# A gated-convolution and ELU kernel: products of TensorE on 64 rows, two halves side by side

## The chip, the cores and the metric

The kernel runs on one core of one Trainium2 chip. The metric is device microseconds of the whole program; the kernel before takes 1214.82 us, the median of 3 runs.

## What is computed

A softmax-weighted causal convolution over 7 tokens (8 heads of 24 features) and a two-layer network with ELU between the layers, all in float32:

```python
w = softmax(weight_gen, axis=-1)                      # (4, 4096, 8, 7)
x_pad = np.concatenate([zeros(B, 6, D), x], axis=1)   # x: (4, 4096, 192)
conv[b, s, h, :] = sum over k of w[b, s, h, k] * x_pad[b, s + k, h, :]
x = conv.reshape(16384, 192)
h = x @ w_in                                          # w_in (192, 2048)
g = np.where(h > 0, h, np.exp(np.minimum(h, 0)) - 1)
out = g @ w_out                                       # w_out (2048, 192)
```

## The kernel before

The 16384 tokens are cut into 32 blocks of 512 tokens (N = 512), and the 2048 hidden features into 16 f-tiles of 128. So there are 512 steps, each one f-tile of one block. A float32 product is made of fp32r products of high and low parts: each operand is split into hi, its value rounded to fp32r, and lo = value - hi, and hi·hi + hi·lo + lo·hi are summed in PSUM.

`f_tile` holds one step. `mm1` (L560) makes h = w_in·x with five products of 128 rows and 512 columns: of the 192 features 128 (32 from each of four quadrants) lie in `xhi` and `xlo`, three products; the other 64 lie twice in `xd`, once as hi and once as lo, which needs two. Then the ELU: ScalarE makes relu(-h) (L567) and exp (L569), VectorE combines them (L571), ScalarE rounds to `hi` (L574), VectorE subtracts to `lo` (L576). `mm2` (L589) multiplies with w_out, five products again: three into the PSUM bank `acc` (128 output features) and two into `accd` (the other 64, whose hi and lo weights lie side by side, so that the two halves of `accd` are added in the drain). `mm2` of a step follows `mm1` of a step four f-tiles later (`LA = 4`), so that the ELU runs beside other products. `h` has three PSUM banks, `acc` and `accd` two each.

Before a block's products, `chunk` loads x and the convolution's weights (four loads each, for two blocks at a time after the first two) and makes the softmax; `conv` sums the seven taps on GpSimd (blocks 0 and 1 in `summed`, with TensorE adding up in PSUM); `split` transposes the sum on VectorE (two instructions of 512 columns) and makes `xhi`, `xlo`, `xd`. After a block's last product `drain` adds the halves of `accd`, transposes both sums on VectorE and stores them. `weights` decodes the weights from 64-bit words during block 0; the 64 extra rows of w_in are doubled by products with `picks` (L353). `turn_over` keeps TensorE busy with products of the identity at the start.

All of this goes through `Plan`: each operation is a task with an engine, a cost and a due time; `issue` lays the tasks out by due time on a model of the engines and then emits them in the order of their modelled starts. That order is each engine's instruction order, and SP's queue of loads and stores as well. `due1(s)` is the due time of step s.

The order of the steps is blocks 0 and 1 in turns of 8, 4 and 4 f-tiles, then block by block.

Of the kernel before, what the change touches and what calls it, by code (L numbers as in the profile page):

```python
# [22 lines left out]
class Ring:  # L23
# [6 lines left out]
    def new(self):  # L30
        h = Handle(self.make)
# [100 lines left out]
def conv_elu_kernel(  # L132
# [16 lines left out]
    Q = 4  # L149
    A = P // Q  # L150
# [4 lines left out]
    E = DQ - A  # L155
# [3 lines left out]
    J = N // A  # L159
    JH = J // 2  # L160
    NB = T * R // J
    D1 = D - P
    FILL = 24
# [3 lines left out]
    LA = 4  # L167

    sizes = [J, J] + [2 * J] * (T * R // (2 * J) - 1)
    starts = [sum(sizes[:i]) for i in range(len(sizes))]  # L170
    CM = max(sizes)
    chunk_of = {st // J + i: (c, i * J) for c, (st, n) in enumerate(zip(starts, sizes))
                for i in range(n // J)}

    def rows(ap, t0, n):

        return ap.rearrange("(a r) t d -> r a t d", r=R)[t0 // T][:, t0 % T:t0 % T + n]

# [7 lines left out]
    count = const.tile([P, 1], I32, name="count")  # L186
    second = const.tile([P, 1], F32, name="second")


    row = const.tile([P, 1], F32, name="row")  # L190
    rows_i = const.tile([P, 1], I32, name="rows_i")
    ids = const.tile([P, P], I32, name="ids")
    col = const.tile([P, P], F32, name="col")
    picks = [const.tile([P, P], F32, name=f"pick{i}") for i in range(2)]

    WC = 2 * P + D
    W = const.tile([P, NF, 2 * WC], F32R, name="W")
    D_HI, A_HI, O_HI, O_BOTH, A_LO, O_LO, D_LO = (slice(c, c + P) for c in range(0, 7 * P, P))  # L200
    in_pieces = {0: 2, 2: 2, **{f: 4 for f in range(4, NF, 4)}}
# [4 lines left out]
    r_raw_in = ring("raw_in", [P, 6 * P, 2], 3, I32)  # L206
    r_m_in = ring("m_in", [P, 6 * P], 2, I32)
    r_raw_out = ring("raw_out", [P, 2 * D, 2], 4, I32)
    r_m_out = ring("m_out", [P, 2 * D], 3, I32)
    r_xw = ring("xw", [P, HALO + CM, DQ], 2)  # L210
    r_wg = ring("wg", [P, CM, H, K], 2)
    r_wm = ring("wm", [P, CM, H, 1], 1)
    r_ws = ring("ws", [P, CM, H, 1], 1)
    r_pa = ring("pa", [P, J, H, G], 2)
    r_pb = ring("pb", [P, J, H, G], 1)
    r_v = ring("v", [P, JH, H, G], 6)
    r_xc = ring("xc", [P, J, H, G], 2)
    r_xt = ring("xt", [P, 2, J * A], 1)
    r_xhi = ring("xhi", [P, N], 2, F32R)
    r_xlo = ring("xlo", [P, N], 2, F32R)  # L220
    r_xd = ring("xd", [P, N], 2, F32R)
    r_xr = ring("xr", [P, N], 1, F32R)
    r_e = ring("e", [P, N], 3)
    r_hi = ring("hi", [P, N], 4, F32R)
    r_lo = ring("lo", [P, N], 4, F32R)
    r_cr = ring("cr", [D1, N], 1)
    r_ot = ring("ot", [P, J, A], 2)
    r_od = ring("od", [D1, J, A], 2)
    r_h = ring("h", [P, N], 3, pool=ps)
    r_wd = ring("wd", [P, 4, P], 1, pool=ps)  # L230
    r_acc = ring("acc", [P, N], 2, pool=ps)
    r_accd = ring("accd", [P, N], 2, pool=ps)
# [4 lines left out]
    idle = r_acc.new()  # L237
# [21 lines left out]
    STEP = 10 * pe(N)  # L259
    T0 = 20000  # L260

    def due1(s):
        return T0 + s * STEP


# [3 lines left out]
    def weights(f0, nf, of_in, own_q=None):  # L269


        raw, m = (r_raw_in.new(), r_m_in.new()) if of_in else (r_raw_out.new(), r_m_out.new())
        hi_h, lo_h = Handle(), Handle()
        fs = W[:, f0:f0 + nf]
        wide = P if of_in else D
        na = nf * wide
        nh = nf // 2
        n = na + (nh * P if of_in else 0)
        for f in range(f0, f0 + nf):
            (w_in_h if of_in else w_out_h)[f] = [hi_h, lo_h]  # L280

        def m_(c=slice(0, n)):
            return m.t[:, c]

        def mf(c=slice(0, n)):
            return m_(c).bitcast(F32)

        def own(c):
            return mf(slice(0, na)).rearrange("p (f m) -> p f m", f=nf)[:, :, c]
# [4 lines left out]
        def load_out():  # L294
            nc.sync.dma_start(
                out=raw.t[:, 0:na].rearrange("p (f m) w -> p f (m w)", f=nf),
                in_=moe_w_out.bitcast(I32)[f0 * P:(f0 + nf) * P, :].rearrange(
                    "(f p) m -> p f m", p=P))

        w = moe_w_in.bitcast(I32).rearrange("(q e) m -> q e m", q=Q)  # L300

        def load_in(eng):
            for q in range(Q):
                eng.dma_start(
                    out=raw.t[q * A:(q + 1) * A, 0:na].rearrange("p c w -> p (c w)"),
                    in_=w[q, 0:A, 2 * f0 * P:2 * (f0 + nf) * P])

        def load_rest():
            for i in range(2):
                at = f0 + i * nh  # L310
                nc.sync.dma_start(  # L311
                    out=raw.t[i * D1:(i + 1) * D1, na:n].rearrange("p c w -> p (c w)"),
                    in_=w[:, A:DQ, 2 * at * P:2 * (at + nh) * P])

        if not of_in:
            add("dma", max(dma(nf * P, 8 * D), ISSUE), load_out, writes=[raw])
        elif own_q:

            begun = Handle()
            add("pool", Q * 1000, lambda: load_in(own_q), writes=[raw, begun])  # L320
            add("dma2", 0, lambda: None, reads=[begun], writes=[raw])
            add("dma", max(dma(P, nh * 8 * P), 2 * ISSUE), load_rest, writes=[raw])
        else:
            add("dma", max(dma(P, 8 * na), Q * ISSUE), lambda: load_in(nc.sync), writes=[raw])
            add("dma", max(dma(P, nh * 8 * P), 2 * ISSUE), load_rest, writes=[raw])
# [17 lines left out]
        if of_in:  # L343
            wd, d_hi, d_lo = r_wd.new(), Handle(), Handle()
            for f in range(f0, f0 + nf):
                w_in_h[f] += d_hi, d_lo

            def wds():
                return wd.t[:, 0:nf]

            def pick():
                for i in range(2):
                    nc.tensor.matmul(out=wd.t[:, i * nh:(i + 1) * nh], lhsT=picks[i],  # L353
                                     rhs=mf(slice(na, n)), start=True, stop=True)

            add("pe", 2 * 4 * pe(nh * P), pick, reads=[m], writes=[wd], due=due1(f0) - 2000)
            add("act", act(nf * P, True), lambda: nc.scalar.copy(out=fs[:, :, D_HI], in_=wds()),
                reads=[wd], writes=[d_hi])
            add("dve", dve(nf * P), lambda: nc.vector.tensor_tensor(
                out=fs[:, :, D_LO], in0=wds(), in1=fs[:, :, D_HI].bitcast(F32), op=ALU.subtract),  # L360
                reads=[wd, d_hi], writes=[d_lo])
        to = A_HI if of_in else slice(O_HI.start, WC)
        add("act", act(na), lambda: nc.scalar.copy(out=fs[:, :, to], in_=own(slice(0, wide))),
            reads=[m], writes=[hi_h])
        parts = ((slice(0, P), A_HI, A_LO),) if of_in else (
# [336 lines left out]
```

## Time and profile before

| | us |
|---|---|
| median of 3 runs | 1214.82 (1213.92 to 1215.94) |
| span of the profiled execution, first to last instruction | 1212.2 |
| TensorE products busy | 1196.1 (99%) |
| TensorE weight loads busy (beside the products) | 984.2 (81%) |
| ScalarE busy | 927.8 (77%) |
| VectorE busy | 898.4 (74%) |
| GpSimd busy | 710.1 (59%) |

A record of a TensorE product is longer than its pace: products are pipelined, and each record begins before its predecessor's has ended. The pace is the distance between starts. A weight load is a record of its own (PEld). Between the profiled span and the median lie 2.6 us.

### The profile page before, as it was taken

How to read it: one execution, taken by the hardware profiler on the slowest of the kernel's cores; microseconds unless marked ns; L12 is line 12 of the kernel's file. 1: busy time of each engine (PE TensorE's matmuls, PEld its weight loads, DVE VectorE, ACT ScalarE, POOL GpSimd, SP SyncE). 2: the span in 40 equal slices, each digit the busy share in tenths (PEclk: the TensorE clock that was granted, in tenths of full speed). 3: DMA queues.
4: the chain of work that ended last, by engine and by line, in shares of the span. 5: the costliest groups of instructions: out<-in, count | busy, mean ns of one | idle time of the engine just before them, and what ended most of it. 6: DMA issues, size and time to landing. Idle time of an engine off the chain costs nothing.

```text
span 1212.2 us, 15948 instructions
## 1 busy us (share of the span) xinstructions
PE 1196.1 (99%) x5268; PEld 984.2 (81%) x5268; DVE 898.4 (74%) x1411; ACT 927.8 (77%) x1716; POOL 710.1 (59%) x442
## 2 busy tenths in 40 slices
PE   8999999999999999999999999999999999999997
PEld 7687888888888888888888888787888888888886
DVE  7977777777787776777677786777777677777765
ACT  5887878777777777777777787777777777787775
POOL 4678393863919458292764909459292774909500
PEclk9999999999999999999999999999999999999999
DMA  7820404004040320404003040220403104000001
GB/s 157 140 33 14 53 14 52 14 10 44 14 52 14 38 28 1 52 14 52 15 13 40 14 52 14 31 31 6 52 14 47 20 9 44 14 14 14 14 9 18
DMA packets 251514, 38.66 MB, mean 32 GB/s; under 512 B 248168, under 2 KB 250472, under 8 KB 251432
## 3 DMA queue, kind: packets, MB, share of 16 engines
q1 hardware_dynamic: 251304, 37.39, 23.1%
q8 instruction: 41, 0.67, 0.2%
q14 instruction: 41, 0.34, 0.1%
q0 software_dynamic: 128, 0.26, 0.1%
HBM read 25.05 MB, written 12.58 MB: 31 GB/s over the span
## 4 chain that ended last, share of the span: by engine, by line
PE 94%; DMA 3%; DVE 1%; SPq 1%; ACT 1%; issue 1%; ACTq 0%
PE h L560 47%; PE acc L589 28%; PE accd L589 19%; DMA raw_in<-in_moe_w_in 2%; SPq L403 1%; DMA xw<-in_x 1%; DVE xd L547 0%; ACT e L567 0%; SPq L311 0%; DVE xlo L547 0%; ACT hi L574 0%; ACT e L569 0%; DVE lo L576 0%; ACT xhi L542 0%; DVE h L571 0%
## 5 line engine op out<-in xcount | busy, mean ns | idle before, releaser
L576 DVE TENSOR_TENSOR lo<-h,hi 128x512 fp32r<-128x512 f32 x512 | 353.8, 691 | 239.1 <-ACT hi L574 195.5
L567 ACT ACTIVATE e<-h 128x512 f32<-128x512 f32 x512 | 307.5, 601 | 158.8 <-PE h L560 157.1
L560 PE MATMUL h<-xd,W 128*128 128x512 f32 x1024 | 401.0, 392 | 4.9 <-DVE xd L547 4.1
L589 PE MATMUL acc<-hi,W 128*128 128x512 f32 x1024 | 399.4, 390 | 0.0
L560 PE MATMUL h<-xhi,W 128*128 128x512 f32 x1024 | 398.5, 389 | 0.0
L571 DVE SCALAR_TENSOR_TENSOR h<-e,h 128x512 f32<-128x512 f32 x512 | 351.9, 688 | 59.2 <-ACT e L569 59.0
L574 ACT CAST hi<-h 128x512 fp32r<-128x512 f32 x512 | 298.8, 584 | 94.0 <-DVE h L571 92.9
L569 ACT ACTIVATE e<-e 128x512 f32<-128x512 f32 x512 | 328.2, 641 | 4.5
L434 POOL TENSOR_TENSOR pb<-xw,wg 128x768 f32<-128x768 f32 x182 | 287.3, 1578 | 11.5
L449 POOL TENSOR_TENSOR pa<-pa,pb 128x768 f32<-128x768 f32 x150 | 282.1, 1880 | 11.7
L434 POOL TENSOR_TENSOR pa<-xw,wg 128x768 f32<-128x768 f32 x32 | 49.5, 1548 | 371.6 <-DVE wg L424 366.2
L560 PEld LDWEIGHTS h<-xd,W 128*128 128x128 f32 x1024 | 192.2, 188 | 48.7 <-DVE xd L547 5.8
L589 PEld LDWEIGHTS acc<-hi,W 128*128 128x128 f32 x1024 | 192.3, 188 | 40.0
L560 PEld LDWEIGHTS h<-xhi,W 128*128 128x128 f32 x1024 | 192.3, 188 | 39.8
L589 PE MATMUL accd<-hi,W 128*128 128x512 f32 x512 | 199.5, 390 | 0.6 <-POOL W L370 0.6
L560 PE MATMUL h<-xlo,W 128*128 128x512 f32 x512 | 199.2, 389 | 0.0
L589 PE MATMUL accd<-lo,W 128*128 128x512 f32 x512 | 199.2, 389 | 0.0
L589 PE MATMUL acc<-lo,W 128*128 128x512 f32 x512 | 199.2, 389 | 0.0
L589 PEld LDWEIGHTS accd<-hi,W 128*128 128x128 f32 x512 | 96.1, 188 | 21.7 <-POOL W L370 1.8
L560 PEld LDWEIGHTS h<-xlo,W 128*128 128x128 f32 x512 | 96.1, 188 | 20.0
L589 PEld LDWEIGHTS accd<-lo,W 128*128 128x128 f32 x512 | 96.1, 188 | 20.0
L589 PEld LDWEIGHTS acc<-lo,W 128*128 128x128 f32 x512 | 96.1, 188 | 20.0
(81 smaller groups left out, 514.3 us busy)
## 6 DMA issues: line engine op xcount, KB each, us to landing
xw<-in_x SPq DMA_DIRECT2D x60, 228.0 KB, 4.9
out_dram<-ot SPq DMA_DIRECT2D x128, 64.0 KB, 2.0
out_dram<-od SPq DMA_DIRECT2D x64, 64.0 KB, 1.9
wg<-in_weight_gen SPq DMA_DIRECT2D x60, 56.0 KB, 3.0
raw_out<-in_moe_w_out SPq DMA_DIRECT2D x8, 384.0 KB, 7.1
raw_in<-in_moe_w_in SPq DMA_DIRECT2D x18, 128.0 KB, 5.1
xw<-in_x SPq DMA_DIRECT2D x8, 132.0 KB, 4.5
raw_in<-in_moe_w_in SPq DMA_DIRECT2D x8, 64.0 KB
```

Of the source, the lines that this page charges most:

```text
L403: nc.sync.dma_start(out=to()[q * A:(q + 1) * A], in_=rows(src, t0, n)[:, :, q * d:(q + 1) * d])
L434: lambda: eng.tensor_tensor(out=h.t, in0=xw.t[:, j0 + k:j0 + k + J, :].rearrange("p j (h g) -> p j h g", g=G), in1=wg.t[:, j0:j0 + J, :, k ...
L449: add("pool", pool(J * DQ), lambda b=b, to=to: nc.gpsimd.tensor_tensor(out=to.t, in0=a.t, in1=b.t, op=ALU.add), reads=[b] if to is a else ...
L560: nc.tensor.matmul(out=h.t, lhsT=W[:, f, w], rhs=r.t, start=(i == 0), stop=(i == len(pairs) - 1))
L567: add("act", act(N, True), lambda: nc.scalar.activation(out=e.t, in_=h.t, func=ACTF.Relu, scale=-1.0), reads=[h], writes=[e])
L569: add("act", act(N), lambda: nc.scalar.activation(out=e.t, in_=e.t, func=ACTF.Exp, scale=-1.0), writes=[e])
L571: add("dve", dve(N), lambda: nc.vector.scalar_tensor_tensor(out=h.t, in0=e.t, scalar=-1.0, in1=h.t, op0=ALU.add, op1=ALU.max), reads=[e], ...
L574: add("act", act(N, True), lambda: nc.scalar.copy(out=hi.t, in_=h.t), reads=[h], writes=[hi])
L576: add("dve", dve(N), lambda: nc.vector.tensor_tensor(out=lo.t, in0=h.t, in1=hi.t.bitcast(F32), op=ALU.subtract), reads=[h, hi], writes=[lo])
L589: nc.tensor.matmul(out=to.t, lhsT=W[:, f, w], rhs=r.t, start=(first and r is hi and w != O_LO), stop=(last and r is lo), skip_group_check= ...
```

## The change

There are no full-array products with w_in any more. A block's 512 tokens are laid out as two halves of 256: the lower 64 partitions hold the 192 features (as `C = 3` parts of 64 rows) of the first half, the upper 64 those of the second. Copies by DMA in `split` (`other`) bring each half's tokens to the other partitions too, so that each half of the rows has all 512 columns. The f-tiles go in pairs: one f-tile's w_in lies on the lower rows, the other's on the upper rows (`WI`), and each f-tile takes nine products of 64 rows (3 terms x 3 parts). The doubled rows, `picks` and `xd` go.

In blocks 0 and 1 the nine products of one f-tile alternate with those of the other, and w_out's ten products per pair stay full. From block 2 on (`APART`) w_out's product is cut in two by its 128 hidden rows: the upper 64 rows' half (`up`) runs two pairs later beside the w_in products of the pair's lower f-tile, the lower half (`down`) three pairs later beside those of the upper f-tile. Each half has its own banks `acc` and `accd`, one of each per half where there were two for all; `drain` runs once per half, with two transposes each, and the halves are added on GpSimd, as are the two halves of `accd`. `h` has four banks, `hi` and `lo` seven buffers. x and the convolution's weights are loaded block by block, in eight pieces each. The planner's step is a pair of f-tiles of 19 product costs. The diff, cut to its core:

```diff
-    Q = 4
-    A = P // Q
+    Q, S = 2, 2
+    A = P // (Q * S)
...
-    E = DQ - A
+    C = DQ // A
...
-    LA = 4
...
+    LAG = 2
+    APART = range(2, NB)
...
+    WI = const.tile([P, NP, 2, C, P], F32R, name="WI")
+    WO = const.tile([P, NF, 3 * P], F32R, name="WO")
...
+    r_xw = ring("xw", [P, HALO + J, DQ], 3)
+    r_wg = ring("wg", [P, J, H, K], 3)
...
+    r_xhi = ring("xhi", [P, C, 3, NS], 2, F32R)
+    r_xlo = ring("xlo", [P, C, 3, NS], 2, F32R)
...
-    r_hi = ring("hi", [P, N], 4, F32R)
-    r_lo = ring("lo", [P, N], 4, F32R)
...
-    r_h = ring("h", [P, N], 3, pool=ps)
...
-    r_acc = ring("acc", [P, N], 2, pool=ps)
-    r_accd = ring("accd", [P, N], 2, pool=ps)
+    r_hi = ring("hi", [P, N], 7, F32R)
+    r_lo = ring("lo", [P, N], 7, F32R)
+    r_cr = ring("cr", [D1, S * J, A], 1)
+    r_h = ring("h", [P, N], 4, pool=ps)
+    r_acc = [ring(f"acc{i}", [P, N], 1, pool=ps) for i in range(2)]
+    r_accd = [ring(f"accd{i}", [P, N], 1, pool=ps) for i in range(2)]
...
-    STEP = 10 * pe(N)
+    STEP = 19 * pe(N)
...
+                for p, s, q in quadrants():
+                    nc.sync.dma_start(out=to()[p],
+                                      in_=rows(src, t0 + s * J, n)[:, :, q * d:(q + 1) * d])
...
+            for c in range(C):
+                def turn(i=i, c=c, xc=xc):
...
+                    nc.vector.transpose(out=xt(i)[:, c], in_=src[:, :, c * A:(c + 1) * A])
+                add("dve", dve(n * A), turn, reads=[xc], writes=[xts[i], part], due=due)
+            done = Handle()
+            add("act", act(C * n * A), lambda i=i: nc.scalar.copy(out=to(xhi, i), in_=xt(i)),
+                reads=[xts[i], part], writes=[xhi, done])
+            add("dve", dve(C * n * A), lambda i=i: nc.vector.tensor_tensor(
+                out=to(xlo, i), in0=xt(i), in1=to(xhi, i).bitcast(F32), op=ALU.subtract),
+                reads=[xts[i], part, done], writes=[xlo], port=blk > 0)
+        low, high = slice(0, HALF), slice(HALF, P)
+        for x in (xhi, xlo):
+            def other(x=x):
+                t = x.t.bitcast(I32)
+                nc.sync.dma_start(out=t[high, :, 0], in_=t[low, :, 1])
+                nc.sync.dma_start(out=t[low, :, 2], in_=t[high, :, 1])
+            add("dma", max(dma(P * C, 4 * NS), 2 * ISSUE), other, writes=[x])
...
+    def product_in(blk, k, i, h):
+        xhi, xlo = xt_h[blk]
+        p, c0 = ((low, 1), (high, 0))[i]
+        terms = [(w, x, c) for w, x in ((1, xhi), (0, xlo), (0, xhi)) for c in range(C)]
+        def one(at):
+            w, x, c = terms[at]
+            return lambda: nc.tensor.matmul(
+                out=h.t, lhsT=WI[p, k, w, c], rhs=x.t[p, c, c0:c0 + 2].rearrange(
+                    "p s n -> p (s n)"), start=(at == 0), stop=(at == len(terms) - 1),
+                skip_group_check=True)
+        return [one(at) for at in range(len(terms))]
+    whole = slice(0, P)
+    def banks(blk, p):
+        return acc_h[blk][1 if p is high else 0]
+    def product_out(blk, k, p):
+        acc, accd = banks(blk, p)
+        out = []
+        for i, f in enumerate(pair_of[k]):
+            hi, lo = elu_h[blk, f]
+            for to, w, r in ((accd, O_BOTH, hi), (accd, O_BOTH, lo), (acc, O_HI, hi),
+                             (acc, O_LO, hi), (acc, O_HI, lo)):
+                def run(f=f, to=to, w=w, r=r, hi=hi, i=i):
+                    nc.tensor.matmul(
+                        out=to.t, lhsT=WO[p, f, w], rhs=r.t[p],
+                        start=(k == 0 and i == 0 and r is hi and w != O_LO),
+                        stop=(k == NP - 1 and i == 1 and r is not hi), skip_group_check=True)
+                out.append(run)
+        return out
...
+    def period(s, now, up, down):
...
+        n = 3 * C
+        if now:
+            blk, k = now
+            h = [r_h.new(), r_h.new()]
+            fs = pair_of[k]
+            reads = [*w_in_h[k], *xt_h[blk]]
+            t0, t1 = (product_in(blk, k, i, h[i]) for i in range(2))
+        if up:
+            blk2, k2 = up
+            if k2 == 0:
+                acc_h[blk2] = [(r_acc[i].new(), r_accd[i].new())
+                               for i in ((1, 0) if blk2 in APART else (blk2,))]
+        if up and up[0] not in APART:
+            if now:
+                add("pe", n * pe(N), run(*pairs(t0, t1)), reads=reads, writes=h, due=due1(s))
+            add("pe", 10 * pe(N), run(*product_out(*up, whole)), reads=ready(blk2, pair_of[k2]),
+                writes=[x for y in acc_h[blk2] for x in y], due=due1(s) + STEP / 2)
+            if now:
+                for f, x in zip(fs, h):
+                    elu(blk, f, x)
+            return
...
+        def side(mine, m2, p, hr, h, at):
+            out = product_out(*m2, p) if m2 else []
+            to = banks(m2[0], p) if m2 else []
+            of = pair_of[m2[1]] if m2 else ()
+            ahead = p is low
+            for a, b, f in ((0, 5, of[0:1]), (5, 10, of[1:2])):
+                todo = [x for i in range(a, b) for x in (
+                    out[i:i + 1] + mine[i:i + 1] if ahead else mine[i:i + 1] + out[i:i + 1])]
+                slots = b - a - (ahead and a == 0)
+                add("pe", slots * pe(N), run(*todo),
+                    reads=[*hr, *(ready(m2[0], f) if m2 else ())],
+                    writes=[*h, *to], due=due1(s) + (at + a) * pe(N))
+        if now:
+            side(t0, up, high, reads, h[0:1], 0)
+            elu(blk, fs[0], h[0])
+            side(t1, down, low, reads, h[1:2], 9)
+            elu(blk, fs[1], h[1])
...
+    def drain(blk, s1, p):
+        late = due1(s1 + 5)
+        soon = due1(s1 + 1)
+        sums = sums_h.setdefault(blk, [])
+        for acc, accd in [banks(blk, p)]:
+            each = []
+            for src in (accd, acc):
+                o = r_raw_out.new(by_token)
+                add("dve", dve(N), lambda o=o, src=src: nc.vector.transpose(
+                    out=o.t.rearrange("p j c -> p (j c)"), in_=src.t),
+                    reads=[src], writes=[o], due=soon)
+                each.append(o)
+            sums.append(each)
+        if p is high:
+            return
+        od, ot = sums[0]
+        for other in sums[1:]:
+            for to, o in zip((od, ot), other):
+                add("pool", pool(N), lambda to=to, o=o: nc.gpsimd.tensor_tensor(
+                    out=to.t, in0=to.t, in1=o.t, op=ALU.add), reads=[o], writes=[to], port=True,
+                    due=late)
+        cr = r_cr.new()
+        add("act", act(N), lambda: nc.scalar.copy(out=cr.t, in_=od.t[D1:P]),
+            reads=[od], writes=[cr], due=late)
+        add("pool", pool(N), lambda: nc.gpsimd.tensor_tensor(
+            out=od.t[0:D1], in0=od.t[0:D1], in1=cr.t, op=ALU.add), reads=[cr], writes=[od],
+            port=True, due=late)
+...
+    cuts = (0, 4, 6, NP)
+    runs = [(blk, k0, k1) for k0, k1 in zip(cuts, cuts[1:]) for blk in range(2)]
+    runs += [(blk, 0, NP) for blk in range(2, NB)]
+    todo = [(blk, k) for blk, k0, k1 in runs for k in range(k0, k1)]
...
+        for s in range(len(todo) + LAG + 1):
+            now = todo[s] if s < len(todo) else None
+            up = todo[s - LAG] if LAG <= s < len(todo) + LAG else None
+            down = todo[s - LAG - 1] if s > LAG else None
+            if down and down[0] not in APART:
+                down = None
...
+            period(s, now, up, down)
+            if up and up[1] == NP - 1:
+                drain(up[0], s, high if up[0] in APART else whole)
+            if down and down[1] == NP - 1:
+                drain(down[0], s, low)
```

## Rows read from the trace of the kernel before

**Rows 1.** The page: busy time by engine, and the ended-last chain by line.

```profile
PE 1196.1 (99%) x5268; PEld 984.2 (81%) x5268; DVE 898.4 (74%) x1411; ACT 927.8 (77%) x1716; POOL 710.1 (59%) x442
...
PE h L560 47%; PE acc L589 28%; PE accd L589 19%; DMA raw_in<-in_moe_w_in 2%; SPq L403 1%; DMA xw<-in_x 1%; DVE xd L547 0%; ACT e L567 0%; SPq L311 0%; DVE xlo L547 0%; ACT hi L574 0%; ACT e L569 0%; DVE lo L576 0%; ACT xhi L542 0%; DVE h L571 0%
```

**Rows 2.** Timeline, TensorE, near 600 us (start us, length us, engine line op).

```profile
600.05 0.39 PE L560 MATMUL h<-xhi,W 128*128 128x512 f32 x1
600.27 0.39 PE L560 MATMUL h<-xlo,W 128*128 128x512 f32 x1
...
602.31 0.39 PE L560 MATMUL h<-xhi,W 128*128 128x512 f32 x1
```

**Rows 3.** Groups by line and form, TensorE (count, busy us, mean ns, idle before).

```profile
L589 PE MATMUL acc<-hi,W 128*128 128x512 f32 x1024 | 399.4, 390 | 0.0
...
L353 PE MATMUL wd<-m_in,pick 128*128 128x256 f32 x12 | 3.1, 379 | 0.0
```

**Rows 4.** Busy time per stretch, engines in the order PE, PEld, DVE, ACT, POOL; clock.

```profile
400.00:600.00 200.00, 200.00 (x884) 165.68 (x883) 147.23 (x230) 155.34 (x289) 114.10 (x68) 1.00 0.24 30
```

**Rows 5.** All waits of TensorE (total us, times, longest).

```profile
PE h L560 <- DVE xd L547: 4.1, 4, 2.3
PE acc L485 <- DVE v L497: 2.6, 2, 1.7
PE acc L378 <- POOL ident masks.py:199: 1.4, 1, 1.4
PE h L560 <- DVE lo L576: 0.8, 1, 0.8
PE accd L589 <- POOL W L370: 0.6, 2, 0.4
```

**Rows 6.** Timeline, TensorE, the fillers and the first w_in product.

```profile
18.03 2.84 PE L378 MATMUL acc<-ident 128*128 128x128 f32 x24
20.63 0.49 PE L560 MATMUL h<-xd,W 128*128 128x512 f32 x1
```

**Rows 7.** Timeline, weight loads, of the same stretch.

```profile
17.92 2.76 PEld L378 LDWEIGHTS acc<-ident 128*128 128x128 f32 x24
20.62 0.19 PEld L560 LDWEIGHTS h<-xd,W 128*128 128x128 f32 x1
20.73 0.19 PEld L560 LDWEIGHTS h<-xhi,W 128*128 128x128 f32 x1
```

**Rows 8.** Timeline, weight loads, near 600 us.

```profile
600.05 0.19 PEld L560 LDWEIGHTS h<-xlo,W 128*128 128x128 f32 x1
```

**Rows 9.** Timeline, SP, the first issues.

```profile
0.75 1.97 SPq L403 DMA_DIRECT2D wg<-in_weight_gen  x4
2.76 2.54 SPq L403 DMA_DIRECT2D xw<-in_x  x4
```

**Rows 10.** Groups by line and form, VectorE and GpSimd.

```profile
L608 DVE STREAM_TRANSPOSE ot<-acc 128x512 f32<-128x512 f32 x32 | 22.7, 709 | 1.9 <-PE acc L589 1.9
...
L370 POOL TENSOR_TENSOR W<-m_in,W 128x512 fp32r<-128x512 f32 x3 | 3.9, 1296 | 0.0
...
L538 DVE STREAM_TRANSPOSE h<-acc 128x256 f32<-128x256 f32 x2 | 0.8, 444 | 0.3 <-PE acc L485 0.3
```

**Rows 11.** The page: DMA issues (count, KB each, us to landing).

```profile
out_dram<-od SPq DMA_DIRECT2D x64, 64.0 KB, 1.9
```

**Rows 12.** Timeline, last product and last store.

```profile
1205.23 0.39 PE L589 MATMUL acc<-lo,W 128*128 128x512 f32 x1
...
1208.44 1.00 SPq L615 DMA_DIRECT2D out_dram<-od  x2
```

**Rows 13.** Timeline, VectorE, a block's second subtract in `split`.

```profile
615.23 2.26 DVE L547 TENSOR_TENSOR xd<-xt,xr 128x512 fp32r<-128x512 f32 x1
```

**Rows 14.** Timeline, last product of an f-tile's h and the end of its ELU.

```profile
609.79 0.39 PE L560 MATMUL h<-xhi,W 128*128 128x512 f32 x1
...
613.55 0.68 DVE L576 TENSOR_TENSOR lo<-h,hi 128x512 fp32r<-128x512 f32 x1
```

More of the change, by code (lines that the diff above doesn't have):

```diff
@@ L184, in conv_elu_kernel @@
     scratch = const.tile([P, 1], F32, name="scratch")
[L186 to L199, printed above, removed]
@@ L257, in dma, with due1, decoded @@
         return packets * max(9 + byts / 12, 22) / 16
-    STEP = 10 * pe(N)
+    STEP = 19 * pe(N)
     T0 = 20000
-    def due1(s):
-        return T0 + s * STEP
+    def due1(k):
+        return T0 + k * STEP
     w_in_h, w_out_h = {}, {}
[L269 to L289, printed above, removed]
+    def decoded(raw, m, n):
@@ L291, in word @@
         def word(i):
             return raw.t[:, 0:n, i]
[L294 to L325, printed above, removed]
+        def m_():
+            return m.t[:, 0:n]
@@ L342, in weights @@
             out=m_(), in0=m_(), in1=word(0), op=ALU.add), reads=[raw, tail], writes=[m])
[L343 to L361, printed above, removed]
@@ new lines, in weights_out, with load, own @@
+    def weights_out(fs):
+        raw, m = r_raw_out.new(), r_m_out.new()
+        hi_h, lo_h = Handle(), Handle()
+        for f in fs:
+            w_out_h[f] = [hi_h, lo_h]
+        f0, step, nf = fs[0], fs[1] - fs[0], len(fs)
+        n = nf * D
+        to = WO[:, f0:fs[-1] + 1:step]
+        def load():
+            nc.sync.dma_start(
+                out=raw.t[:, 0:n].rearrange("p (f m) w -> p f (m w)", f=nf),
+                in_=moe_w_out.bitcast(I32).rearrange("(f p) m -> p f m", p=P)[
+                    :, f0:fs[-1] + 1:step])
+        add("dma", max(dma(nf * P, 8 * D), ISSUE), load, writes=[raw])
+        mf = decoded(raw, m, n)
+        def own(c):
+            return mf().rearrange("p (f m) -> p f m", f=nf)[:, :, c]
+        add("act", act(n), lambda: nc.scalar.copy(out=to[:, :, 0:D], in_=own(slice(0, D))),
@@ L533, in turn @@
                     src = src[:, 0:n * DQ].rearrange("p (j d) -> p j d", d=DQ)
-                    if i == 0:
-                        src = src[:, :, 0:A]
-                    else:
-                        src = src[:, :, A:DQ].unsqueeze(2).to_broadcast([P, n, 2, E])
-                    nc.vector.transpose(out=xt(i)[:, j * n * A:(j + 1) * n * A], in_=src)
-                add("dve", dve(n * A), turn, reads=[xc], writes=[xts[i], h], due=due)
-        add("act", act(N), lambda: nc.scalar.copy(out=xhi.t, in_=xt(0)),
-            reads=[xts[0], parts[0]], writes=[xhi])
@@ L578, in f_tile @@
             reads=[h, hi], writes=[lo])
-        if first:
-            acc_h[blk] = r_acc.new(), r_accd.new()
-        acc, accd = acc_h[blk]
-        def mm2():
-            for to, w, r in ((acc, O_HI, hi), (accd, O_BOTH, hi), (acc, O_LO, hi),
-                             (accd, O_BOTH, lo), (acc, O_HI, lo)):
-                nc.tensor.matmul(
-                    out=to.t, lhsT=W[:, f, w], rhs=r.t, start=(first and r is hi and w != O_LO),
-                    stop=(last and r is lo), skip_group_check=True,
-                )
```

283 lines of the change are left out of this document (143 added, 140 removed).

## The prediction

> **What bounds the kernel now.** I read the busy shares and the chain that ended last first: TensorE is busy 99% of the span, and the two product lines L560 and L589 carry 94% of the chain [rows 1]. The reader is to see that no other engine and no queue has a share that matters. The timeline then gives the price of one product: a product of w_in and the same one of the next f-tile, ten products later, stand 2.26 us apart, and neighbours 0.22 to 0.23 [rows 2]. Over a 200 us stretch 884 products lie without a gap, which is 226.2 ns each by count; I take 226.7 ns, the pace that longer gap-free stretches of the timeline keep (the recorded 390 ns of one is its length with the pipeline, not its pace [rows 3]). The granted clock is 1.00 there, the 2.4 GHz level [rows 4], so no part of the price is a throttle. The waits of TensorE come to 9.4 us in all [rows 5]. So time is the number of product places times 226.7 ns, plus what lies at the two ends: 5120 x 0.2267 = 1160.7 us of 1212.2, and 51.5 us for the start, the weights' picking, a few waits and the tail.
>
> **What the change takes away.** An f-tile costs 5 + 5 full products now. After it, w_in needs nine 64-row products per f-tile (three 64-row parts of the 192 rows, three hi/lo terms) in place of five of 128 rows of which one was only half new work; w_out's ten per pair of f-tiles become twenty 64-row ones. If a low-half and a high-half product share one place, a pair of f-tiles takes (18 + 20) / 2 = 19 places, not 20. Blocks 0 and 1 take 9 pairs and 10 full products, 19 too. That is 256 x 19 = 4864 places, and about 10 more where a half runs alone (w_in at the entry into block 2, w_out at the very end): 4874, of which 4704 are pairs. At 226.7 ns this is 1104.9 us, 55.8 us less. The 20 picking products go as well, 12 of them recorded with 379 ns [rows 3], some 3 us at their pace.
>
> **The pace of a pair** is the disputed price, and no row shows a pair. Below: two weight loads and two issues have to fit in one place. The 24 fp32 fillers at the start take 2.60 us to the next product, 108 ns for each load and product [rows 6], and the loads alone stand 108 to 112 ns apart; the first fp32r load is followed by the next after 0.11 us [rows 7]. Two make 217 ns, under 226.7, so neither issue nor loading should bind, and 217 is the lower end (-10.1 ns x 4704 = -47.5 us). Above: if the halves ran one after another, 453 ns. I take 226.7, one place of today, because today's matmul and the next load already run side by side [rows 2, 7 and 8] and loads of two halves still fit under it; the pace of a single stream stays what it is. Break-even against all other terms is worked out below.
>
> A load on the same 128 rows starts together with the matmul that precedes it, at 600.05 in both rows [rows 2 and 8], so weights are fetched while the rows work. The Trainium skill ("TensorE: Matmul & The Clock Gate", Part 3, The mechanism) says that weight loads overlap running matmuls only where the row group differs; it speaks against the change, since alternate products share a half with the one two before. By the trace this does not hold for a full array; by the rule it is the third rival.
>
> **What it adds.** Each switch between 64-row pairs and full products in blocks 0 and 1, 34 of them: at most the pipeline's 390 - 227 = 163 ns [rows 3], 5.6 us, at least nothing; I take 5, the upper end being nearest to a drain. (The Trainium skill, "TensorEngine Tiling (Array Packing)", Key Properties, says that changing the tiling mode drains TensorE; no row here shows a switch, and the sum stands without the sentence.)
>
> The start: loads of x and the weights of the convolution are issued in 8 pieces each, not 4; four of them hold SP 1.97 and 2.54 us [rows 9], so x comes up to 4.5 us later. Then the first block's turn is two transposes longer (0.44 us each [rows 10]), and two copies per tensor across the halves follow on SP, issue and landing some 3 us by the stores' 1.9 us landing [rows 11]. Up to 8.4 us; part of that falls into the stretch where products wait for weights anyway, so between 0 and 8.4, taken as 6.
>
> The tail: today 3.2 us lie between the last product and the last store [rows 12]. The halves are to be added on GpSimd, three adds near 1.30 us each [rows 10], partly beside the last transposes: 1 to 4 us more, taken as 2.
>
> In steady state the copies of a block ride on SP, which has 34 us per block for some 26 issues of about 0.5 us. What is queued behind a copy that waits for VectorE's subtract is the next loads and the stores; these have a block's time to spare. GpSimd gets 3 x 1.3 us per block on a load of 114 of 200 us [rows 4]: about 0.57 x 36.3 + 3.9 = 24.6 of 34.5 us. VectorE has 147 of 200, 26.7 us per block; it gains one transpose of 709 ns [rows 10] and the second set of short softmax steps, loses about half a microsecond in the split, and comes to some 27.5 of 34.5, 80% (estimate). ScalarE stays near 28 us, 81%.
>
> What is next late: the ELU chain. From the last product of an f-tile (609.79) to the end of lo it takes 613.55 + 0.68 - 610.18 = 4.05 us [rows 14]. Today the h bank, three f-tiles deep, grants 3 x 2.267 - 1.13 = 5.67 us. After the change the second f-tile of a pair is wanted one period and five places later, 4.31 + 1.13 = 5.44 us, the first 6.5. So the cover shrinks by a little and holds unless VectorE is blocked; one subtract of 512 columns took 2.26 us while GpSimd worked [rows 13], and it is to become one of 768. And the sums have one bank each: after the last product of a half into accd its next block writes 12 places on, 2.7 us, in which two transposes (1.42 us), the pipeline (0.16) and perhaps one running VectorE instruction (0.69) must pass: 2.3 us. It fits by 0.4. For both I add 4 us; bounds 0 and 36 (0.6 us twice in 30 blocks).
>
> **Sum.** 1104.9 + 51.5 - 3 + 5 + 6 + 2 + 4 = 1170.4 us of span. The median of the runs stands 2.6 us above the profiled span (1214.8 against 1212.2), so 1173 us, 3.4% faster. Break-even is 41.8 us / 4704 = 8.9 ns: a pair at 235.6 ns gives all back.
>
> **Rivals.**
> First, slower: the weight loads of the two halves take turns, and each holds the array longer than half a place. It begins to cost at 113.4 ns a load and ends the gain at 117.8. For it: a load is recorded with 188 ns [rows 8]; at 2 x 188 = 376 ns a pair, 4704 x 149.3 ns make 1875 us. Against: loads 108 to 112 ns apart [rows 7]. A milder form, 240 to 250 ns a pair, gives 4704 x 13.3 to 23.3 ns more, 1236 to 1283 us. Chance 0.11.
>
> Second, the change doesn't do what it says: the halves run one after another, 4704 x 226.7 ns more, 2239 us. Nothing in the trace excludes it. Chance 0.09.
>
> Third, a half's next weights wait until that half's matmul is through (the skill's rule above): 108 + 227 = 335 ns a pair, 4704 x 108.3 ns more, 1682 us. Against it stands 600.05 [rows 2 and 8]. Chance 0.03.
>
> Fourth, the pairs run, but the drains and the blocked subtract stall TensorE at each block's end by the upper bounds: 1173 + 32 = 1205, up to 1225 if both meet. For it: 0.4 us of margin and 2.26 us [rows 13]; against: only 9.4 us of waits today with similar slack [rows 5]. Chance 0.12.
>
> Fifth, a pair is limited by loads alone, 217 ns: 1173 - 47.5 = 1125 us. Chance 0.08.
>
> **How the numbers follow.** My forecast, pairs at one place's pace with small stalls (1145 to 1197 us), has 0.57: predicted 1173. The range 1120 to 1230 takes in the fifth, the fourth and the mildest form of the first, and leaves out about 0.2, all above it. Faster by over 0.2% (about what a measurement of this kernel can tell from no change) are the forecast, the fifth and two thirds of the fourth: 0.73. Within 0.2%: 0.03, from the fourth and the mild first. Slower: 0.24.
>
> **What would show it.** Low-half and high-half products in the records starting at most a place apart in pairs, 38 of them in 4.3 us: right. 38 in 4.5 us or more: the first rival; in 8.6: the second; in 6.4: the third. Waits of w_out's products on the drain's transposes, or of w_in on lo, above 0.5 us per block: the fourth. First product later than 29 us, or over 9 us after the last, would show the start and the tail too small. It is wrong as a whole if a pair takes over 235.6 ns.

## The result and the profile after

| | us, median | ratio to before, 95% interval | span of the profiled execution |
|---|---|---|---|
| before | 1214.37 | 1 | 1212.2 |
| after | 1198.41 (1197.54 to 1202.26) | 0.9874 [0.9857, 0.9892] | 1200.5 |
| predicted | 1173 (1120 to 1230) | 0.966 | 1170.4 |

The change makes the kernel 1.3% faster. The direction and the range hold; the size does not: 16 us came of the 42 that were forecast. The profiled execution of after is the longest of its four (1202.26 us), 3.9 us above their median.

The page of after has the same bound as before [rows 1]: TensorE busy 98%, its two product lines (now L555 for w_in, L577 for w_out) 86% of the chain that ended last. The second line is that chain, share of the span by line, from which the small shares at its end can be left aside.

```profile
PE 1179.1 (98%) x9696; PEld 936.5 (78%) x9696; DVE 913.6 (76%) x1504; ACT 950.1 (79%) x1714; POOL 833.4 (69%) x535
...
PE h L555 41%; PE acc L577 27%; PE accd L577 18%; POOL pb L420 1%; POOL pa L435 1%; POOL raw_out L700 1%; PE accd L471 1%; PE acc L471 1%; DMA xw<-in_x 1%; DVE lo L597 0%; SPq L389 0%; POOL pa L420 0%; ACT e L590 0%; DVE m_in L286 0%; ACT e
```

The waits of TensorE (total us, times, longest) stand against [rows 5]. All but one lie in the start and in blocks 0 and 1. The one is the last line here, from the timeline: in block 2 a group of products waits 0.99 us for lo, the end of an ELU. No drain holds a product up.

```profile
PE acc L471 <- DVE v L483: 4.3, 2, 2.9
PE h L555 <- DVE lo L597: 3.6, 3, 1.5
PE accd L577 <- ACT e L590: 3.3, 1, 3.3
PE acc L367 <- POOL ident masks.py:199: 1.4, 1, 1.4
PE h L555 <- POOL WI L328: 0.5, 1, 0.5
...
151.82 0.49 PE L555 MATMUL h<-xhi,WI 64*128 64x512 f32 x1 [0.99 <-DVE lo L597]
```

The timeline of TensorE near 600 us (start us, length us) stands against [rows 2]. A product of a w_in half and one of a w_out half start within 0.01 us of each other: the halves do run side by side. But the line of 599.45 comes again at 603.88, one pair of f-tiles (19 places) later: 4.43 us, 233.3 ns a place, not 226.7.

```profile
599.44 0.40 PE L577 MATMUL acc<-lo,WO 64*128 64x512 f32 x1
599.45 0.62 PE L555 MATMUL h<-xhi,WI 64*128 64x512 f32 x2
599.68 0.39 PE L577 MATMUL accd<-hi,WO 64*128 64x512 f32 x1
599.91 0.40 PE L555 MATMUL h<-xhi,WI 64*128 64x512 f32 x1
599.91 0.40 PE L577 MATMUL accd<-lo,WO 64*128 64x512 f32 x1
...
603.88 0.62 PE L555 MATMUL h<-xhi,WI 64*128 64x512 f32 x2
```

The row of the 200 us stretch, columns as in [rows 4], says the same without a gap: 1718 records, 859 pairs of which some two lie across the edges, in 200 us; and the granted clock is 1.00, so the lost 6.6 ns are no throttle.

```profile
400.00:600.00 200.00, 200.00 (x1718) 160.58 (x1716) 156.10 (x256) 163.37 (x294) 148.08 (x91) 1.00 0.32 57
```

From the last switch to 64-row products (128.48, the third pair of f-tiles of block 2) to the start of the last product (1192.00) lie 1063.5 us. By the program's order these are 4552 places: 238 pairs of f-tiles of 19 places, and 30 with w_out's products alone. At 233.3 ns their 4551 distances make 1061.9 us, and 1.6 us are the wait in block 2 and shorter breaks. At 226.7 they would make 1031.6: 30 us, the whole miss of this execution (1200.5 us of span for 1170.4). The question of the experiments is therefore one term, the pace of a pair.

### The profile page after: what moved, and what is told of

It reads as the page before. It is cut to its first block, busy times and chain, and to the rows that moved or that the text cites. A ratio compares the mean times of both kernels' runs of the same rounds, so it can differ in the third digit from the quotient of the medians.

```text
span 1200.5 us, 25349 instructions
## 1 busy us (share of the span) xinstructions
PE 1179.1 (98%) x9696; PEld 936.5 (78%) x9696; DVE 913.6 (76%) x1504; ACT 950.1 (79%) x1714; POOL 833.4 (69%) x535
## 4 chain that ended last, share of the span: by engine, by line
PE 88%; issue 6%; POOL 3%; DVE 1%; ACT 1%; DMA 1%; SPq 0%; POOLq 0%; DVEq 0%
PE h L555 41%; PE acc L577 27%; PE accd L577 18%; POOL pb L420 1%; POOL pa L435 1%; POOL raw_out L700 1%; PE accd L471 1%; PE acc L471 1%; DMA xw<-in_x 1%; DVE lo L597 0%; SPq L389 0%; POOL pa L420 0%; ACT e L590 0%; DVE m_in L286 0%; ACT e L588 0%
## 5 line engine op out<-in xcount | busy, mean ns | idle before, releaser
L555 PE MATMUL h<-xhi,WI 64*128 64x512 f32 x3072 | 812.4, 393 | 4.3 <-DVE lo L597 3.6
L577 PE MATMUL acc<-hi,WO 64*128 64x512 f32 (+1 forms) x1984 | 616.9, 392 | 0.0
L555 PEld LDWEIGHTS h<-xhi,WI 64*128 64x128 f32 x3072 | 544.8, 184 | 81.4 <-DVE lo L597 6.6
L555 PE MATMUL h<-xlo,WI 64*128 64x512 f32 x1536 | 425.1, 392 | 0.0
L577 PEld LDWEIGHTS acc<-hi,WO 64*128 64x128 f32 (+1 forms) x1984 | 364.6, 185 | 47.1
L577 PE MATMUL accd<-hi,WO 64*128 64x512 f32 (+1 forms) x992 | 389.8, 395 | 3.3 <-ACT e L590 3.3
L577 PE MATMUL accd<-lo,WO 64*128 64x512 f32 (+1 forms) x992 | 387.6, 392 | 0.1
L577 PE MATMUL acc<-lo,WO 64*128 64x512 f32 (+1 forms) x992 | 387.1, 392 | 0.0
L555 PEld LDWEIGHTS h<-xlo,WI 64*128 64x128 f32 x1536 | 273.8, 184 | 35.2
L577 PEld LDWEIGHTS accd<-hi,WO 64*128 64x128 f32 (+1 forms) x992 | 182.2, 184 | 31.8 <-POOL WO L359 4.1
L577 PEld LDWEIGHTS accd<-lo,WO 64*128 64x128 f32 (+1 forms) x992 | 182.4, 185 | 23.2 <-DVE lo L597 0.5
L577 PEld LDWEIGHTS acc<-lo,WO 64*128 64x128 f32 (+1 forms) x992 | 182.1, 184 | 23.4
```

The lines of the kernel that those rows point to most:

```text
L555: return lambda: nc.tensor.matmul(out=h.t, lhsT=WI[p, k, w, c], rhs=x.t[p, c, c0:c0 + 2].rearrange("p s n -> p (s n)"), start=(at == 0), s ...
L577: nc.tensor.matmul(out=to.t, lhsT=WO[p, f, w], rhs=r.t[p], start=(k == 0 and i == 0 and r is hi and w != O_LO), stop=(k == NP - 1 and i == ...
```

## The experiments

Paces are worked out from the starts of the matmul records, over a stretch without gaps. Kernels that only time products store zeros and compute nothing of the reference.

**1. What a 64-row product costs by itself.**

```diff
+for i in range(60):          # one half alone; then the other; then pairs, as here
+    matmul(out=bank[0], lhsT=w[low, i % 8], rhs=r[low])
+    matmul(out=bank[3], lhsT=w[high, i % 8], rhs=r[high])
```

> Nothing of the task is computed here: 60 products of each kind follow one another on TensorE, and the distance between starts is read for each kind. Theory A, a 64-row fp32r product has a longer pace than a full one whether or not another half runs: one half alone 231 to 233 ns, pairs 233, full 226.7. Theory B, only the second product of a pair costs: one half alone 226.7, pairs 233. Theory C, two weight loads per place bind: pairs of 256 columns near 217 ns, and pairs with 64 columns of weights back at 226.7. If the addition is fixed per place, full products of 256 columns take 120 ns and pairs 126; if it goes with the columns, 120 and 123. Full and pairs in turns: 0.2 us more per switch, as the trace after shows. Two of one half and then two of the other: 233 per pair by A and B.

TensorE's timeline of this run: 60 full products, then 54 in a row of one half alone.

```profile
21.77 13.76 PE L54 MATMUL bank<-r,w 128*128 128x512 f32 x60
...
49.11 12.42 PE L61 MATMUL bank<-r,w 64*128 64x512 f32 x54
```

(13.76 - 0.39) / 59 = 226.6 ns for a full product, (12.42 - 0.39) / 53 = 227 for one half alone, and pairs settle at 226.7 too, after some ten places of 224 to 236. Four quarters of 32 rows share a place of 226.7 as well. Ten full products and nine pairs in turns take 4.78 us where 19 places are 4.31: 0.24 us a switch, with nothing to wait for. Products of 256 columns take 120 ns, full or in pairs. Pairs with 64 columns of weights settle at 229.5 ns, which none of the theories had and which was not followed up. For weights of 128 columns, then, neither a 64-row product, nor the second one beside it, nor two weight loads cost anything here, and the three theories fall. What makes the pair of the kernel dearer is something that this kernel lacks.

**2. Only w_in in pairs, w_out in full products everywhere.**

```diff
-    APART = range(2, NB)
+    APART = range(0)
```

> One part of the change alone: w_in in 64-row pairs everywhere, w_out full everywhere (as in blocks 0 and 1). Theory: each switch between 64-row and full products costs about 0.225 us, as the periods of 4.82 us in blocks 0 and 1 show against 4.36 of their places. 240 more periods with two switches each are 108 us, less 240 x 10 full places that are 6.1 ns shorter (15 us): 1291 us. Rival, switches cost at most the pipeline's 163 ns and the rest of those periods was weights and waits: 1198 + 78 - 15 = 1261 us; if switches were free, 1184 us.

1289.54 us, ratio 1.0615 [1.0584, 1.0646], as reckoned from switches. A period is 4.82 us in place of 4.43, and holds two switches between 64-row pairs and full products. So pairs for w_in alone would make the kernel slower than before; the change gains only because w_out goes in halves beside them.

**3. The lower half's w_out products left out in six of a block's eight pairs of f-tiles.**

```diff
     def product_out(blk, k, p):
+        if p is low and 0 < k < NP - 1:
+            return out
```

> Left out: the lower 64 rows' half of the product with w_out in pairs 1 to 6 of each block's eight, from block 2 on. The places stay 19 per pair of f-tiles; in 9 to 10 of them one half now runs alone. Theory A (a 64-row product is longer by itself): lone places 231 ns instead of 232.8, 180 x 10 x 1.7 ns = 3 us less, 1195 us. Theory B (the second product of a pair costs the 6.1 ns): lone places 226.7, 11 us less, 1187 us. If the halves did not really share their places, half the time of these places would go: 180 x 10 x 116 ns = 210 us less.

1196.35 us, ratio 0.9848 [0.9819, 0.9877]: 1800 products fewer, and a time that the interval does not tell from the changed kernel's. Between 400 and 600 us a place takes 232.5 ns, although in about four of ten one half runs alone; from one of these to the next it is 232.3 ns. So places are really shared, and in this kernel a half without a partner is as slow as a pair.

**4. Offsets between the halves, order, sums, several moving operands.**

```diff
+matmul(out=bank[3][:, 0:256], lhsT=w[high, 0], rhs=r[high, 0:256])   # upper 120 ns late
+for i in range(90): one product of the lower half, one of the upper
```

> Nothing of the task is computed here: seven stretches of 90 pairs of 64-row products (lower, upper, lower, upper), each behind 16 full products. e1 showed a half alone and a settled pair at 226.67 ns, the pace of a full product, so theories A, B and C of e1 are gone. What is left is theory D: the pace of a pair depends on how far apart its halves start. In the kernel they start 3 to 4 ns apart and a pair takes 233; in e1 the upper half led by 14 to 16 ns and it took 226.67. Expected by D: stretch 1 (no offset) 229 to 233 throughout; stretches 2 to 4 (one half delayed by a product of 256 or 64 columns) drift to an offset of 10 ns or more and then stay at 226.67, at least where the upper half is the one that leads. Stretch 5, where one half gets two products in turn every tenth place as in the kernel: stays off 226.67 if the swapping undoes the drift, else 226.67. Stretches 6 and 7 sum in PSUM with seven moving operands, with and without offset: as 3 and 1 if the addresses don't matter. Rival F, addresses and sums in PSUM make the difference and the offset doesn't: 6 and 7 both near 233, 1 to 5 all settle at 226.67.

All seven stretches settle at 226.7 ns within some ten places. In the timeline the line of 29.80 comes again twenty places later, at 34.33, which is 226.5 ns by these rounded starts.

```profile
29.80 0.39 PE L63 MATMUL bank<-r,w 64*128 64x512 f32 x1
...
34.33 0.39 PE L63 MATMUL bank<-r,w 64*128 64x512 f32 x1
```

The theories of the offset and of the sums fall. The first places after a switch between full products and halves, though, are 335, 235, 234, 236, 224, 231, 236, 228, 233, 231 ns, and the last nine of these have a mean of 232, about as slow as the kernel's. The slow pace is something that a switch starts and that ends here, but not there.

**5 to 8. Tiles on multiples of 64 bytes.** All tiles of after that lie behind `scratch` start 32 bytes beside such a multiple. The edits widen a small tile ahead of them (all moved), move it behind the weights (weights moved alone), or add one between (moving operands moved alone). The last run widens the same tile in the kernel before.

```diff
-    scratch = const.tile([P, 1], F32, name="scratch")
+    scratch = const.tile([P, 16], F32, name="scratch")
```

> The changed kernel with one tile made longer: scratch takes 64 bytes of each partition, not 4 (which are rounded to 32), so that every tile behind it starts at a multiple of 64 bytes, where it starts 32 bytes behind one now. e4 had all tiles at multiples of 64 and settled at 226.67 ns in every stretch, sums and changing operands or not, while the kernel stays at 233.3 in a 229/237 pattern. Theory G: the start addresses of the operands make the difference; pairs go back to 226.7 and 4704 x 6.6 ns = 31 us fall away: 1167 us. Rival H, the other engines' work in SBUF and PSUM makes it (e4 had none): 1198 us, unchanged.

> scratch placed behind the two weight tiles: WI and WO start at multiples of 64 bytes, the moving operands stay 32 bytes behind one. By G with the weights as the part that matters 1167 us; with the moving operands as that part 1198 us; by H 1198 us.

> A 32-byte tile behind the weights: the moving operands (xhi, xlo, hi, lo) start at multiples of 64 bytes, WI and WO stay 32 bytes behind one. By G with the moving operands as the part that matters 1167 us; with the weights as that part 1198 us; by H 1198 us. If both parts cost, e6 and e7 share the 31 us.

> The kernel before with the same longer scratch, all tiles at multiples of 64 bytes. Its full products take 226.67 ns with the tiles 32 bytes off, the pace of e1 and e4 with aligned tiles; so by G and H alike nothing changes: 1214.5 us, within 0.2%.

| | us, median | ratio | pace of a place, ns (profiled execution) |
|---|---|---|---|
| all moved | 1199.99 | 0.9891 [0.987, 0.9913] | 232.4 |
| weights alone | 1206.99 | 0.9945 | 234.3 |
| moving operands alone | 1205.10 | 0.9929 | 234.3 |
| before, all moved | 1212.87 | 0.9996 [0.9985, 1.0006] | 226.7 |

Alignment to 64 bytes is not it. Yet moving one kind of operand against the other by 32 bytes, whichever of the two is moved, changes the pace by the same 1 to 2 ns, and moving both does not make it worse. This was the trail.

**9. The kernel's own tiles, without the other engines.**

```diff
+stretch(10)                                   # WI, WO, xhi, xlo, hi, lo, banks, order as in the kernel
+stretch(5, w="one")                           # one piece of weights; then one operand, one bank, ...
+plain(95)                                     # plain pairs beside ScalarE, VectorE, GpSimd at work
```

> Nothing of the task is computed: zeros are stored, and TensorE runs stretches of 64-row products with tiles of the same names, shapes and addresses as in the changed kernel, each stretch behind 16 full products. Stretch 1: ten periods of 19 places exactly as in the changed kernel (same pieces of WI and WO, same xhi, xlo, hi and lo tiles, same banks, same sums, same order), with the other engines idle. 2: one piece of weights for all. 3: one moving operand for all. 4: one bank for each half. 5: the lower half issued first throughout. 6: one piece, one operand, one bank. 7: no sums. 8 to 13: plain lockstep pairs while ScalarE copies in SBUF, ScalarE copies from PSUM, VectorE adds in SBUF, VectorE adds from PSUM, GpSimd adds in SBUF, and all three at once. Theory H (the other engines' traffic holds the pairs at 233 ns): 1 to 7 settle at 226.7 ns a pair, and at least one of 8 to 13 stays near 233. Theory I (the operands hold them: their places, banks or order): 1 stays at 233.3 ns, the one of 2 to 7 that takes the cause away settles at 226.7, and 8 to 13 settle at 226.7. Theory J (the waits between the engines hold them): all stretches settle at 226.7.

All thirteen stretches stay slow, at 232.4 ns, and so do the 16 full products between them. In the timeline, two lines 38 places apart: 8.82 / 38 = 232.1 ns, with every other engine idle.

```profile
59.43 0.61 PE L63 MATMUL h<-xhi,WI 64*128 64x512 f32 x2
...
68.25 0.61 PE L63 MATMUL h<-xhi,WI 64*128 64x512 f32 x2
```

That all stayed slow was expected by none of the three theories, and is what solved it. Traffic, waits, banks, order and sums are out, and so is the pair: full products are as slow. What is left, common to all these stretches and absent from experiments 1 and 4, is where the tiles lie. By the addresses of the programs as built, in the kernel after WI begins at byte 17056 of a partition, WO at 41632 and xhi at 126752; from any piece of weights to any moving operand it is a multiple of 512 bytes and 128 more. In the kernel before, W at 19232 and xhi at 138272, it is a multiple of 512 and 256 more. In experiments 1 and 4 it is a plain multiple of 512 for the fp32r tiles. Below, this remainder is called the distance.

**10. The distance between weights and moving operand by itself.**

```diff
+off = [sb.tile([P, N + 8], F32R, name=f"off{32 * i}_") for i in range(16)]   # 32 bytes further each
+for m in off: 32 x matmul(lhsT=w[:, i % 8], rhs=m[:, 0:N]); then 32 pairs of 64 rows
```

> Nothing of the task is computed: zeros are stored, and TensorE runs stretches of 32 products (full, then 64-row pairs) for each of 16 moving tiles, whose addresses lie 0, 32, 64, ... 480 bytes beyond a multiple of 512 bytes counted from the weights; then the same with weights that lie 128 bytes further on, halves at two distances, and two distances in turns. Theory K (the distance in bytes between moving operand and weights, modulo 256 or 512, sets the pace, of full products as of pairs; the changed kernel's is 128, the kernel before's 256, that of the earlier stretches of pairs that settled 0): 226.7 ns at the distances 0 and 256, some 232 ns at 128 and 384, for full products as for pairs; with the weights 128 bytes on, 226.7 moves to the tile at 128. Rival L (the distance has no part in it): one pace, 226.7, in all stretches.

TensorE's timeline, 32 full products in a row (start, length); off__64 is the tile at distance 0, and each number more is 32 bytes more. w__80 are weights that lie 128 bytes further on.

```profile
31.21 7.52 PE L62 MATMUL bank<-off__64,w 128*128 128x512 f32 x32
46.95 7.71 PE L62 MATMUL bank<-off__65,w 128*128 128x512 f32 x32
63.09 7.59 PE L62 MATMUL bank<-off__66,w 128*128 128x512 f32 x32
95.14 7.69 PE L62 MATMUL bank<-off__68,w 128*128 128x512 f32 x32
111.23 7.74 PE L62 MATMUL bank<-off__69,w 128*128 128x512 f32 x32
159.69 7.51 PE L62 MATMUL bank<-off__72,w 128*128 128x512 f32 x32
223.64 7.69 PE L62 MATMUL bank<-off__76,w 128*128 128x512 f32 x32
288.19 7.68 PE L73 MATMUL bank<-off__64,w__80 128*128 128x512 f32 x32
304.27 7.54 PE L73 MATMUL bank<-off__68,w__80 128*128 128x512 f32 x32
```

Distances 0 and 256 are the short ones, 128 and 384 are 0.17 us longer. The last two lines show that it is the distance and not the place: with the weights 128 bytes on, the tile at 128 is the fast one and that at 0 the slow one. The settled pace (mean of the last 16 intervals), by distance modulo 256:

| bytes | 0 | 32 | 64 | 96 | 128 | 160 | 192 | 224 |
|---|---|---|---|---|---|---|---|---|
| full, ns | 226.6 | 233.3 | 228.9 | 233.2 | 232.2 | 234.3 | 233.4 | 233.4 |
| pairs, ns | 226.6 | 233.4 | 228.9 | 233.6 | 232.1 | 234.3 | 233.4 | 233.3 |

The 234.3 of experiments 6 and 7, at distance 160, stands here too.

**11. The changed kernel at distance 0.** 384 unused bytes behind the weights, nothing else.

```diff
     WO = const.tile([P, NF, 3 * P], F32R, name="WO")
+    const.tile([P, 96], F32, name="pad")
```

> The changed kernel with 384 unused bytes behind its weights, so that every moving operand lies a multiple of 512 bytes from its weights; all else is the same. Theory K: pairs go from 233.3 to 226.7 ns, 4552 places of them: 1198 - 30 = 1168 us, ratio about 0.962. Rival L: 1198 us, as the changed kernel.

1172.09 us, ratio 0.9656 [0.964, 0.9672]: 26 us less than the changed kernel, and the best of all. Theory K's 1168 lies 4 us lower: its 30 us are what the profiled executions differ by (1202.26 and 1171.97), and were taken off the median. Row of the stretch, and two lines of the timeline 19 places apart:

```profile
400.00:600.00 200.00, 200.00 (x1768) 165.28 (x1766) 161.50 (x264) 167.88 (x302) 150.29 (x93) 1.00 0.32 57
...
598.88 0.61 PE L556 MATMUL h<-xhi,WI 64*128 64x512 f32 x2
...
603.18 0.61 PE L556 MATMUL h<-xhi,WI 64*128 64x512 f32 x2
```

1768 records against 1718, and 4.30 us for a pair of f-tiles against 4.43: 226.7 ns a place by the unrounded starts. The steady part, from the last switch (128.12) to the last product, takes 1033.6 us, of which 4551 x 226.67 ns are 1031.6; the other 2.0 us are breaks, 1.1 us of them the wait for lo in block 2.

**12. The kernel before at distance 384, 128 modulo 256.**

```diff
     W = const.tile([P, NF, 2 * WC], F32R, name="W")
+    const.tile([P, 32], F32, name="pad")
```

> The kernel before with 128 unused bytes behind its weights, so that the distance of moving operands from weights goes from 256 to 384 bytes beyond a multiple of 512, as far from a multiple of 256 as the changed kernel's 128. Theory K: its full products go from 226.7 to some 232 ns: 1214 + 5200 x 0.0056 = about 1243 us, ratio 1.023. Rival L: 1214 us, no change.

1241.58 us, ratio 1.0227 [1.0211, 1.0243]. 128 unused bytes cost the old kernel 28 us. Its windows (against the 884 products of [rows 4]) show two paces at one distance, 232.4 ns early and 233.3 late:

```profile
400.00:600.00 200.00, 200.00 (x862) 162.14 (x861) 147.78 (x224) 152.57 (x283) 108.96 (x64) 1.00 0.23 28
950.00:1150.00 200.00, 200.00 (x859) 160.91 (x858) 146.10 (x223) 151.00 (x280) 120.72 (x71) 1.00 0.18 23
```

The change comes behind one gap of 307 ns at 855.9 us: until there the distances between starts repeat every seven places (228 to 241 ns), from there 229 and 238 alternate. What sets the pattern stays open. It may be most of the spread of after too, whose executions lie between 1197.5 and 1202.3: 0.95 ns in 4552 places is 4.3 us. That is an estimate; of after only the longest execution was profiled, and it has the 233.3.

## Why the prediction was right or wrong

**The bound and the places: right.** Time went as places times pace. 9408 records of 64 rows are the 4704 pairs of the sum (by the program's order 4694 pairs and 20 products alone), and the 160 full w_out products of blocks 0 and 1 stand beside them. At equal distance the change is worth what the sum said: 0.9656 with both kernels at a multiple of 256, and 1198.41 / 1241.58 = 0.965 with both 128 beside one; forecast was 0.966.

**The pace of a pair: the step that failed.** The sum took "226.7, one place of today, because ... the pace of a single stream stays what it is". The reason against a dearer pair was sound: halves and their loads share a place for nothing (experiments 1, 3 and 11). The error was to take 226.7 for a property of the product. It was one of the kernel before and its layout. The change resizes the buffers that lie between the weights and the moving operands (those of x and the convolution's weights among them), which moved the distance from 256 to 128, and with it the pace from 226.7 to 233.3 ns in the profiled execution: 4551 x 6.66 = 30 us. The range held it only because it was made wide for other causes. A sign lay in the trace of before, which I did not use: after a wait its full products too are slow before they keep 226.7 (behind the wait that ends at 764.5 us, 335 ns and then nine places of 224 to 236), so the pace was no constant even there.

**The other terms**, read from the run at distance 0 (span 1170.2 against 1170.4 forecast), are less exact than their sum. That the sum is met to 0.2 us is luck:

- Start: first 64-row product at 29.53, forecast 20.6 + 6 = 26.6. +2.9 us.
- Switches: 35 and not 34. A period of block 0 takes 4.79 us (54.83 to 59.62) where 19 places are 4.31: 0.24 us a switch, above the upper bound of 0.163. Total 8.4 us for 5, +3.4. The bound took the pipeline's length alone. The timeline of the same run shows the rest: 0.34 us from the first full product to the second, then places of 224 to 236 ns, 232 in the mean, through the run of ten, because every switch starts the slow places again.

```profile
54.83 0.50 PE L578 MATMUL accd<-hi,WO 128*128 128x512 f32 x1
55.17 0.40 PE L578 MATMUL accd<-lo,WO 128*128 128x512 f32 x1
55.40 0.63 PE L578 MATMUL acc<-hi,WO 128*128 128x512 f32 x2
55.87 0.39 PE L578 MATMUL acc<-lo,WO 128*128 128x512 f32 x1
...
59.62 0.50 PE L578 MATMUL accd<-hi,WO 128*128 128x512 f32 x1
```

  The Trainium skill ("TensorEngine Tiling (Array Packing)", Key Properties) says that a change of tiling mode drains TensorE; these rows agree that a switch costs, some 0.11 us for itself.
- Tail: last product at 1161.72, end at 1170.2, 8.5 us against 7.0 before: 1.5 more for 2 forecast.
- Stalls: 2.0 us in the steady part, for 4 forecast (experiment 11).
- What lies in blocks 0 and 1 beside products and switches came out some 4 us smaller than taken over from before. This is what the sum leaves, an estimate.

**Rivals.** Loads in turns and halves in turns did not come: one period takes 4.43 us, not 4.5 or more, nor 8.6. By its own yardstick ("38 of them in 4.3 us: right") the forecast was between, and none of the rivals had a place for it. The third rival's rule, that a load waits for its own half's matmul, did not hold: one half alone keeps 227 ns a product in experiment 1, and [rows 8] had said so of full ones. The stalls at the drain did not come: 0.4 us of margin was enough. The wait on lo, the fourth rival's other sign, came in one block of the 30 from block 2 on, 1.0 us in block 2. Pairs at 217 ns did not come: at the best distance they keep 226.7, like the full products. The first 64-row product, at 29.54 us and so later than 29, showed the start too small, as the prediction's signs had it. The missing rival was a shift of the layout.

## What to carry to other kernels

When an edit changes the size or number of the tiles that lie between weights and moving operand in SBUF, their distance in bytes changes with it, and on a TensorE-bound kernel that alone was worth 2.2 and 2.3% (experiments 11 and 12). For products like these put pad bytes so that it is a multiple of 256, and compare two versions at equal distance. When a pace differs by a few per cent with no wait and a granted clock of 1.00, rebuild the products alone with the same addresses before suspecting the other engines. Row halves do share a place for nothing, but keep the runs between switches of row shape long: 0.24 us each.

## What the runs showed of the hardware

- At distance 0 or 256 modulo 512, products of 512 fp32r columns settle at 226.7 ns, elsewhere at means of 228.9 to 234.3, mostly in repeating patterns (two places long at 192, three at 64, seven at 128; experiment 10). By which mechanism the distance acts is not shown; only fp32r products of 512 columns with 128-column weights were swept. Pairs with 64-column weights took 229.5 ns at distance 0 (experiment 1).
- At one distance two paces occur, 232.4 and 233.3 ns at 128 modulo 256 (experiment 12). Why is open.
- After a wait or a switch the first one to ten places are slow even at distance 0: some 320 to 340 ns and then up to nine of 224 to 236 (experiments 4 and 10).
- With the two halves at different distances, 0 and 128, the one at 0 settled at 227 ns and ran ahead of the other, which took 232 (experiment 10).
- Pairs start 3 to 4 ns apart by the unrounded records; the Trainium skill ("TensorE: Matmul & The Clock Gate", Part 3, Measured speedup vs the span model) gives some 4 ns a tile, and this agrees.
- Four products of 32 rows share a place of 226.7 ns over the 40 places of experiment 1. The Trainium skill ("TensorE: Matmul & The Clock Gate", Part 3, Measured speedup vs the span model) has 3.07 times measured for four row tiles; the four to a place here are more.
- bf16 products of 512 columns took 216 ns in experiment 1, full, half or paired, 10.7 ns less than fp32r in the same run.
